# Windowed attention and spectral mixing on one core: the last 64 tokens of v move from GpSimd's queue to SyncE's, as 512-byte rows that four 0/1 products per batch put in place

## The chip, the cores and the metric

The kernel runs on one core of one Trainium2 chip. The metric is the device time of one execution in microseconds, lower is better. Three runs of the kernel before took 447.61, 448.76 and 446.3 us, median 447.61. The profile is of a further execution of 450.29 us.

## What is computed

Attention with 8 heads of 64 over 8 batches of 576 tokens (q, k, v in float32), each token looking at itself and the 127 before it, with a slope per head; its output, 8 x 576 x 512, goes through a Fourier mix with complex weights per mode, and through one dense layer.

```python
B, H, S, D = 8, 8, 576, 64
scores = q @ k.T / sqrt(D) - slope[h] * |i - j|      # where 0 <= i - j < 128, else -1e9
x = softmax(scores) @ v                              # [8, 576, 512], heads side by side
X = rfft(x, axis=1)[:, :64]                          # 64 modes
Y[m] = X[m] @ (w_r[m] + 1j * w_i[m])                 # 512 x 512 per mode, w_r and w_i in float32
u = x + irfft(Y, n=S)
out = u + relu(u @ w_ch)
```

w_r and w_i are 64 x 512 x 512 float32 each, 134 MB together, and are read once.

## The kernel before, in words

**Units and slots.** The attention is done in 32 units: a unit is one batch `b` and one pair of heads `s`. `GROUPS = ((0,), (1, 2, 3))` orders them: first pair 0 for the eight batches (units 0 to 7, group 0), then pairs 1, 2, 3 for batch 0, batch 1 and so on (units 8 to 31, group 1). `_slot(g, n, ...)` (L589) is one step of a software pipeline: scores of unit n, transposes of unit n + 1 on PE (`_tr`, L413) and their evacuation by ACT (`_evac`, L425), casts of q and k of unit n + 2 and of v of unit n + 1 on POOL (`_cast_qk`, L392; `_cast_v`, L401), the spectrum of unit n - 2 (`_spectrum`, L516), the product with v of unit n - 1 (`_av`, L472), and, from unit 8 + 2 on, products with the weights of group 0 (`_pair_of_modes`, L680). The order of the instructions on each engine is the order in which these functions are called; each engine works through its own list in order and waits where a tile is not ready.

**Tokens 512 to 575.** v's first 512 tokens come per unit, in two transfers of 128 KB with 512-byte rows on SP (`_load_v`, L367), and are cast to bf16 (`vb`). The last 64 tokens of all batches are kept in one tile, `vbt` [128, 4 pairs, 8 batches, 72], bf16: partition 64·hh + p holds head hh of the pair and token 512 + p, and a column of ones that gives the sum of the softmax. Before the change they come per pair: `_load_vt` (L378) issues two transfers of 128 KB on GpSimd's queue, in 256-byte rows, and `_cast_vt` (L388) casts 128 x 512 numbers into `vbt`. Pair 0 is loaded after the first cast of q and k and cast before the first transposes; pairs 1 to 3 are loaded in slots 2 to 4 and cast in slots 4 to 6 (L613 to L619). `_av` reads `vbt` in its last two products (L499).

**Loads.** Everything else is issued by SP in one list: q and k of a unit (`_load_unit`, L355, 288 KB each), v of a unit, and weights (`_load_w`, L645). Up to n = 15 this list is written out ahead of everything (L126 to L134): v for units 0 to 4 with their q and k, then v three units behind, and two weight transfers after each unit from 7 on. Later q, k and v are issued from the slots, and weights by `_modes` (L687) as soon as the ring has room. The ring is 12,288 floats per partition, 6 MB: twelve transfers of 512 KB (group 0: 2 modes, 128 rows, w_r or w_i, 64 transfers in all), or four of 1.5 MB (group 1: 384 rows). A transfer needs the room that PE has done with. A transfer also waits until the one eight places ahead of it in SP's list has landed. q and k have 9 buffers each, v 6, vt 2.

**After the attention.** PE goes through the weights of group 1 in order (`_modes`, L704), with the products `u @ w_ch` (`_xw`, L749) and the inverse transform (`_z_early`, L768) between them; `_finish` (L848) puts the results together and writes them out.

**PSUM.** `tqk` of pool `ps1`, two buffers, holds the transposes; `_tr` takes one for q and one for k in each slot:

```python
tp = g.ps1.tile([P, g.R, 64], BF16, tag="tqk", name=f"tqk{w}")
```

**Start.** POOL makes the identity and a few index tiles (`_consts`, L243), DVE makes the distance tile `rel` from them, and ACT the masks (`_mask`, L308), which must be there before the first product with the mask (L464).

Of the kernel before, what the change touches and what calls it, by code (L numbers as in the profile page):

```python
# [9 lines left out]
FP32 = mybir.dt.float32  # L10
BF16 = mybir.dt.bfloat16
# [5 lines left out]
P = 128  # L17
MB = 8
GROUPS = ((0,), (1, 2, 3))
# [4 lines left out]
VB = 6  # L24
# [20 lines left out]
def kernel(  # L45
# [10 lines left out]
    nc = tc.nc  # L56
    B, H, S, D = q.shape
# [4 lines left out]
    g = Ctx()  # L62
# [27 lines left out]
    for b in range(B):  # L90
        t = [(g.x_sb[:, b, st], ((b, st * P), (b, st * P + 64))) for st in range(4)]
        if b % 2:
            t.append((g.x4[:, b // 2], ((b - 1, 4 * P), (b, 4 * P))))
        if b == B - 1:
            t = [t[4], t[1], t[0], t[3], t[2]]
        g.seq += t

    with tc.manual_schedule(engines={ET.SP, ET.PE, ET.Activation, ET.DVE, ET.Pool}):
        with ExitStack() as wctx:
# [5 lines left out]
            with ExitStack() as actx:  # L105
                cp = actx.enter_context(tc.tile_pool(name="const", bufs=1))
                g.Xn[0] = cp.tile([P, 1, 2, B, NM], BF16, name="Xn0")
                g.sel[0] = g.sel[1]
                if JOINT[0] != 2:
                    g.sel[0] = cp.tile([P, JOINT[0], JOINT[0], P], BF16, name="sel0")  # L110
                g.mask = cp.tile([P, NP, 2, 512], BF16)
                g.vbs = [cp.tile([P, 8, 72], BF16, name=f"vb{i}") for i in range(3)]
                g.vbt = cp.tile([P, NP, B, 72], BF16)
                g.qpool = actx.enter_context(tc.tile_pool(name="qk", bufs=QK))
                g.vpool = actx.enter_context(tc.tile_pool(name="v", bufs=VB))
                g.vts = actx.enter_context(tc.tile_pool(name="vts", bufs=2))
                g.work = actx.enter_context(tc.tile_pool(name="work", bufs=2))
                g.ps2 = actx.enter_context(
                    tc.tile_pool(name="ps2", bufs=1, space=bass.MemoryType.PSUM))
                g.ps1 = actx.enter_context(  # L120
                    tc.tile_pool(name="ps1", bufs=2, space=bass.MemoryType.PSUM))
                g.pss = actx.enter_context(
                    tc.tile_pool(name="pss", bufs=1, space=bass.MemoryType.PSUM))

                n0 = g.first[1] + LA
                for n in range(n0):  # L126
                    _load_unit(g, n)
                    if n < VB - 1:
                        _load_v(g, n)
                    elif n >= VB + 2:  # L130
                        _load_v(g, n - 3)
                    if n >= g.first[1] - 1:
                        for _ in range(4 // JOINT[0]):
                            _load_w(g)  # L134
                with tc.tile_pool(name="tmpc", bufs=1, side="right") as tp:
                    _consts(g, tp)
                    _cast_qk(g, 0)
                    for s in GROUPS[0]:
                        _load_vt(g, s)
                    _cast_qk(g, 1)  # L140
                    _cast_v(g, 0)
                    for s in GROUPS[0]:
                        _cast_vt(g, s)
                    _tr(g, 0, 0)
                    _tr(g, 0, 1)
                    _evac(g, 0, 0)
                    _evac(g, 0, 1)
                    first = dict.fromkeys(u[1] for u in units[:2])
                    rest = [s for s in range(NP) if s not in first]
                    for s in first:  # L150
                        _mask(g, tp, s)
                    for n in range(3):
                        _slot(g, n, [], [])
                    for s in rest:
                        _mask(g, tp, s)
                zx = ctx.enter_context(tc.tile_pool(name="zx", bufs=1, side="right"))
                g.ZTa = zx.tile([P, NM // 16, 4, 2, 16, 8], FP32)
                loaded = n0

                work = {n: [] for n in range(N + 2 + TAIL)}  # L160
                for j in range(len(GROUPS) - 1):
                    steps = []
                    for n in range(g.first[j + 1] + 2, g.first[j + 2] + 2):
                        steps += [n] * (SHARE if n < N - LA else SHARE_END)
                    if j + 2 == len(GROUPS):
                        steps += [n for n in range(N + 2, N + 2 + TAIL)] * SHARE_END
                    steps.sort()
                    for m in range(0, NM, JOINT[j]):
                        work[steps[m * len(steps) // NM]].append((j, m))
                for j in set(JOINT):  # L170
                    _sel_rows(g, JOINT.index(j))
                for n in range(3, N + 2 + TAIL):
                    if g.first[1] <= n and loaded < N + 3:
                        if loaded < N:
                            _load_unit(g, loaded)
                        _load_v(g, loaded - 3)
                        loaded += 1
                    w = work[n]
                    h = (len(w) + 1) // 2
                    _slot(g, n, w[:h], w[h:])  # L180
# [62 lines left out]
def _consts(g, tp):  # L243
    nc = g.nc
# [12 lines left out]
    for vb in g.vbs:  # L257
        nc.gpsimd.memset(vb[:, :, g.D : g.D + 1], 1.0)
    nc.gpsimd.memset(g.vbt[:, :, :, g.D : g.D + 1], 1.0)


    pcol = tp.tile([P, 1], FP32)
# [112 lines left out]
            in_=g.v[b, 2 * s + hh, 0:512, :].rearrange("(k p r) d -> p k (r d)", k=2, r=2))  # L375


def _load_vt(g, s):  # L378

    vt = g.vts.tile([P, g.B, g.D], FP32, tag="vt", name=f"vt{s}")  # L380
    for hh in range(2):
        g.nc.gpsimd.dma_start(
            out=vt[64 * hh : 64 * hh + 64],
            in_=g.v[:, 2 * s + hh, 512:576, :].rearrange("b p d -> p b d"))
    g.unit["vt", s] = vt


def _cast_vt(g, s):  # L388
    g.nc.gpsimd.tensor_copy(g.vbt[:, s, :, 0 : g.D], g.unit.pop(("vt", s)))


def _cast_qk(g, n):  # L392
# [196 lines left out]
def _slot(g, n, w0, w1):  # L589


    N = len(g.units)
    if n == g.first[1] + 2:
        _select(g, 0, 0)
    if n < N:
        _score(g, n, 0)
    if n + 1 < N:
        _tr(g, n + 1, 0)
        _evac(g, n + 1, 0)
        _tr(g, n + 1, 1)  # L600
    if n == N + 1:
        _spectrum(g, n - 2)
    for w in w0:
        _pair_of_modes(g, *w)
    if n < N:
        _score(g, n, 1)
    if n + 1 < N:
        _evac(g, n + 1, 1)
    if n + 2 < N:
        _cast_qk(g, n + 2)  # L610
    if n + 1 < N:
        _cast_v(g, n + 1)
    for j, grp in enumerate(GROUPS[1:]):  # L613
        for i, s in enumerate(grp):
            if n == g.first[j + 1] - 4 + i:
                _cast_vt(g, s)
        for i, s in enumerate(grp):
            if n == g.first[j + 1] - 6 + i:
                _load_vt(g, s)  # L619
    if 0 <= n - 2 < N - 1:  # L620
        _spectrum(g, n - 2)
    if 0 <= n - 1 < N:
        _av(g, n - 1)
    if n < N:
        _mask3(g, n)
    for w in w1:
        _pair_of_modes(g, *w)
# [292 lines left out]
```

## Time and profile before

| | |
|---|---|
| median of three runs | 447.61 us (446.3 to 448.76) |
| the profiled execution | 450.29 us |
| its span, first to last instruction of the program | 448.5 us |
| PE / DVE / ACT / POOL busy | 294.1 / 216.1 / 189.6 / 139.1 us |
| moved by DMA | 173.86 MB, 388 GB/s on average |
| of it in POOL's queue (q0, vt) | 1.05 MB |
| granted PE clock, mean | 0.77 |
| vt transfers | 8 of 128 KB, 7.5 us from issue to landing |
| q, k / v transfers | 64 of 288 KB, 6.2 us / 64 of 128 KB, 5.8 us |
| weights | 64 of 1.5 MB (the last one in parts), 13.8 us; 64 of 512 KB, 7.4 to 8.0 us |

How to read it: all times are of one execution and in us from its first instruction. L12 is line 12 of the kernel. The page cuts the span into 40 slices of 11.2 us; a digit is the busy share in tenths. The DMA share is the mean over 16 DMA engines, and can pass 1.0, since the records of packets overlap. "DMA ring<-in_moe_w_r_dram" in a chain is a stretch in which the work waited for that transfer, from its issue to its landing. SPq is SP's list of transfers.

### The profile page before, as it was taken

How to read it: one execution, taken by the hardware profiler on the slowest of the kernel's cores; microseconds unless marked ns; L12 is line 12 of the kernel's file. 1: busy time of each engine (PE TensorE's matmuls, PEld its weight loads, DVE VectorE, ACT ScalarE, POOL GpSimd, SP SyncE). 2: the span in 40 equal slices, each digit the busy share in tenths (PEclk: the TensorE clock that was granted, in tenths of full speed). 3: DMA queues.
4: the chain of work that ended last, by engine and by line, in shares of the span. 5: the costliest groups of instructions: out<-in, count | busy, mean ns of one | idle time of the engine just before them, and what ended most of it. 6: DMA issues, size and time to landing. Idle time of an engine off the chain costs nothing.

```text
span 448.5 us, 12893 instructions
## 1 busy us (share of the span) xinstructions
PE 294.1 (66%) x5506; PEld 204.2 (46%) x5527; DVE 216.1 (48%) x427; ACT 189.6 (42%) x302; POOL 139.1 (31%) x257
## 2 busy tenths in 40 slices
PE   2467989887787885222235664854856748696993
PEld 2455767666666763111123333432433334464661
DVE  8458566566765661010002543453535345462882
ACT  3787656584866741000011331322313233251794
POOL 7699889586876702020000000000000000000700
PEclk9969576686988975555555988589778587899997
DMA  8999999999999999999999999999999999996498
GB/s 249 346 335 327 388 325 353 347 390 379 392 368 375 393 415 429 432 425 426 430 427 433 426 429 429 427 430 426 430 429 430 426 429 430 427 428 282 185 374 288
DMA packets 51562, 173.86 MB, mean 388 GB/s; under 512 B 4912, under 2 KB 21296, under 8 KB 43440
## 3 DMA queue, kind: packets, MB, share of 16 engines
q1 hardware_dynamic: 51120, 171.99, 97.2%
q0 software_dynamic: 384, 1.05, 0.9%
q8 instruction: 43, 0.70, 0.6%
q14 instruction: 15, 0.12, 0.1%
HBM read 163.58 MB, written 9.44 MB: 386 GB/s over the span
## 4 chain that ended last, share of the span: by engine, by line
DMA 50%; PE 26%; ACT 10%; DVE 6%; issue 4%; POOL 2%; ACTq 0%; POOLq 0%
DMA ring<-in_moe_w_r_dram 47%; ACT att L459 6%; PE acc L704 5%; PE sc L447 4%; PE xt L539 4%; PE u L825 3%; PE av L493 3%; DMA ring<-in_moe_w_i_dram 3%; ACT qkT L428 3%; PE tqk L420 2%; PE u L745 2%; POOL qkb L397 1%; PE xw L758 1%; DVE x_sb L507 1%; ACT mask L311 1%
## 5 line engine op out<-in xcount | busy, mean ns | idle before, releaser
L704 PE MATMUL acc<-Xz,ring 128*128 128x32 bf16 x2048 | 70.7, 183 | 100.2 <-DMA ring<-in_moe_w_r_dram 51.0
L704 PEld LDWEIGHTS <-ring 128*128 128x128 bf16 x2048 | 61.3, 101 | 130.1 <-DMA ring<-in_moe_w_r_dram 65.1
L763 ACT CAST hl<-xw 64x512 bf16<-64x512 f32 x72 | 41.7, 579 | 105.6 <-PE xw L758 70.9
L459 ACT ACTIVATE att<-sc 128x1024 bf16<-128x1024 f32 x64 | 65.6, 1025 | 32.8 <-PE sc L447 26.7
L764 DVE TENSOR_TENSOR hl<-xw,hl 64x512 bf16<-64x512 f32 x72 | 49.6, 688 | 58.1 <-ACT hl L763 57.8
L409 POOL CAST vb<-v 64x256 bf16<-64x256 f32 x128 | 64.7, 505 | 20.1 <-PE av L493 13.7
L783 POOL MEMSET ZTa<- 32x512 bf16 x2 | 1.0, 515 | 187.5 <-ACT ZTa L781 187.5
L447 PE MATMUL sc<-qkT,qkT 64*64 64x256 bf16 (+1 forms) x512 | 32.4, 330 | 30.1 <-ACT qkT L428 16.3
L758 PE MATMUL xw<-wch,xT 128*128 128x512 bf16 x138 | 46.3, 467 | 2.7 <-issue 2.2
L428 ACT COPY qkT<-tqk 128x576 bf16<-128x576 bf16 x64 | 40.7, 638 | 0.6 <-PE tqk L420 0.6
L420 PE MATMUL tqk<-ident_b,qkb 64*64 64x64 bf16 x1152 | 31.7, 214 | 7.6 <-POOL qkb L397 6.9
L420 PEld LDWEIGHTS <-qkb 64*64 64x64 bf16 x1152 | 30.8, 130 | 10.2 <-POOL qkb L397 9.2
L464 DVE TENSOR_TENSOR att<-att,mask 128x1024 bf16<-128x1024 bf16 x32 | 26.9, 839 | 14.7 <-ACT att L459 14.5
L585 ACT ACTIVATE Xz<-xz 128x192 bf16<-128x192 f32 (+1 forms) x24 | 7.5, 313 | 59.0 <-DVE Xz L584 57.9
L493 PE MATMUL av<-vb,att 128*128 128x65 bf16 (+1 forms) x512 | 30.8, 215 | 0.6 <-issue 0.2
L584 DVE CAST Xz<-xz 128x384 bf16<-128x384 f32 (+1 forms) x24 | 12.0, 511 | 36.4 <-PE xz L578 35.7
L447 PEld LDWEIGHTS <-qkT 64*64 64x64 bf16 x512 | 13.1, 120 | 35.3 <-ACT qkT L428 18.8
L397 POOL CAST qkb<-k 128x576 bf16<-128x576 f32 x32 | 27.5, 859 | 0.0
L493 PEld LDWEIGHTS <-att 128*128 128x128 bf16 (+1 forms) x512 | 24.4, 111 | 6.5 <-issue 0.6
L397 POOL CAST qkb<-q 128x576 bf16<-128x576 f32 x32 | 24.6, 768 | 6.1 <-PE tqk L420 3.3
L738 DVE COPY xT<-tp 128x512 bf16<-128x512 bf16 x36 | 15.2, 421 | 21.9 <-PE tp L736 21.4
L469 DVE TENSOR_TENSOR att<-att,mask 128x1024 bf16<-128x1024 bf16 x32 | 25.0, 780 | 1.5 <-ACT att L459 1.1
(104 smaller groups left out, 395.2 us busy)
## 6 DMA issues: line engine op xcount, KB each, us to landing
ring<-in_moe_w_r_dram SPq DMA_DIRECT2D x32, 1536.0 KB, 13.8
ring<-in_moe_w_i_dram SPq DMA_DIRECT2D x31, 1536.0 KB, 13.7
ring<-in_moe_w_i_dram SPq DMA_DIRECT2D x33, 512.0 KB, 8.0
ring<-in_moe_w_r_dram SPq DMA_DIRECT2D x32, 512.0 KB, 7.4
q<-in_q_dram SPq DMA_DIRECT2D x32, 288.0 KB, 6.3
k<-in_k_dram SPq DMA_DIRECT2D x32, 288.0 KB, 6.2
v<-in_v_dram SPq DMA_DIRECT2D x64, 128.0 KB, 5.8
out_dram<-o SPq DMA_DIRECT2D x32, 256.0 KB, 3.3
```

Source lines behind the costliest of these rows:

```text
L397: g.nc.gpsimd.tensor_copy(tb, t)
L409: g.nc.gpsimd.tensor_copy(o[64 * r : 64 * r + 64, i], v[64 * i : 64 * i + 64, r])
L420: g.nc.tensor.transpose(tp[hs, r, :], u.b[w][hs, r], g.ident_b[hs, hs], tile_position=(64 * hh, 64 * hh))
L428: g.nc.scalar.copy(dst.rearrange("c (p r) -> c p r", r=g.R), u.tp[w].rearrange("c r p -> c p r"))
L447: nc.tensor.matmul(sc[64 * r : 64 * r + 64, hh, 256 * i : 256 * i + nq], lhsT=kT[hs, c * P + r : c * P + P : 2], rhs=qT[hs, c * P : c * P ...
L459: nc.scalar.activation(a, sc, AF.Exp, scale=1.0 / math.sqrt(g.D))
L464: nc.vector.tensor_tensor(out=a, in0=a, in1=m, op=ALU.mult)
L493: nc.tensor.matmul(av[o, hh, col(t)], lhsT=att[c // 2][:, hh, q0 : q0 + m], rhs=u.vb[:, 2 * c + hh, 0 : D + 1], start=(j == 0), stop=(t < ...
L704: nc.tensor.matmul(acc[:, et, :, m0 - c0 : m0 - c0 + n, :], lhsT=wt[:, a, et * P : (et + 1) * P], rhs=X[:, a, 1 - w : 3 - w, m0 % MB : m0 ...
L758: nc.tensor.matmul(xw, lhsT=xT[:, dt], rhs=g.wch[:, dt], start=(dt == 0 and n in RELU), stop=(dt == 3))
L763: nc.scalar.copy(g.hl[own, n, h], xw[own])
L764: nc.vector.tensor_tensor(out=g.hl[other, n, h], in0=xw[own], in1=g.hl[own, n, h], op=ALU.subtract)
```

## The change

vt comes per batch instead of per pair. `_load_vt(g, b)` issues two transfers of 64 KB on SP, right behind v of the unit with the same number, for b = 0 to 7. Each brings four heads: a row of 512 bytes is two tokens, and lies on partition 4·p + h for tokens 512 + 2p, 512 + 2p + 1 of head h. `_cast_vt(g, b)` casts them to bf16 on POOL (128 x 256 numbers) in slot b, and `_put_vt(g, b)` in slot b + 1 moves them to their places with four products with 0/1 matrices (`selv`, built once by POOL from the identity) into a PSUM tile that takes a `tqk` buffer, from which DVE copies them to `vbt`. `_put_vt` stands ahead of `_spectrum` and `_av` in the slot; `_av` of unit b, in the same slot, is the first to read them. The line numbers of the functions below the change shift by up to 17.

```diff
-                g.vts = actx.enter_context(tc.tile_pool(name="vts", bufs=2))
+                g.vts = actx.enter_context(tc.tile_pool(name="vts", bufs=VB))
+                g.selv = cp.tile([P, 2, 2, P], BF16, name="selv")
...
                     _load_unit(g, n)
-                    if n < VB - 1:
-                        _load_v(g, n)
-                    elif n >= VB + 2:
-                        _load_v(g, n - 3)
+                    for i in [n] * (n < VB - 1) + [n - 3] * (n >= VB + 2):
+                        _load_v(g, i)
+                        if i < B:
+                            _load_vt(g, i)
...
                     _cast_qk(g, 0)
-                    for s in GROUPS[0]:
-                        _load_vt(g, s)
                     _cast_qk(g, 1)
                     _cast_v(g, 0)
-                    for s in GROUPS[0]:
-                        _cast_vt(g, s)
...
+    nc.gpsimd.memset(g.selv, 0.0)
+    src = g.ident_b.rearrange("p (m i h) -> p i h m", i=2, h=2)
+    for r in range(2):
+        for i in range(2):
+            nc.gpsimd.tensor_copy(
+                g.selv[:, i, r].rearrange("p (h m r) -> p r h m", h=2, r=2)[:, r], src[:, i])
...
-def _load_vt(g, s):
-
-    vt = g.vts.tile([P, g.B, g.D], FP32, tag="vt", name=f"vt{s}")
-    for hh in range(2):
-        g.nc.gpsimd.dma_start(
-            out=vt[64 * hh : 64 * hh + 64],
-            in_=g.v[:, 2 * s + hh, 512:576, :].rearrange("b p d -> p b d"))
-    g.unit["vt", s] = vt
-
-
-def _cast_vt(g, s):
-    g.nc.gpsimd.tensor_copy(g.vbt[:, s, :, 0 : g.D], g.unit.pop(("vt", s)))
+def _load_vt(g, b):
+
+    vt = g.vts.tile([P, 2, 2, g.D], FP32, tag="vt", name=f"vt{b}")
+    for i in range(2):
+        g.nc.sync.dma_start(
+            out=vt[:, i].rearrange("p r d -> p (r d)"),
+            in_=g.v[b, 4 * i : 4 * i + 4, 512:576].rearrange("h (p r) d -> p h (r d)", r=2))
+    g.unit["vt", b] = vt
+
+
+def _cast_vt(g, b):
+    t = g.work.tile([P, 2, 2, g.D], BF16, tag="vtb", name="vtb")
+    g.nc.gpsimd.tensor_copy(t, g.unit["vt", b])
+    g.unit["vt", b] = t
+
+
+def _put_vt(g, b):
+
+    t = g.unit.pop(("vt", b))
+    ps = g.ps1.tile([P, 2, 2, g.D], FP32, tag="tqk", name="pvt")
+    for i in range(2):
+        for r in range(2):
+            g.nc.tensor.matmul(
+                ps[:, :, i], lhsT=g.selv[:, i, r], rhs=t[:, :, r], start=(r == 0), stop=(r == 1))
+    g.nc.vector.tensor_copy(
+        g.vbt[:, :, b, 0 : g.D], ps.rearrange("p j i d -> p (j i) d"))
...
-    for j, grp in enumerate(GROUPS[1:]):
-        for i, s in enumerate(grp):
-            if n == g.first[j + 1] - 4 + i:
-                _cast_vt(g, s)
-        for i, s in enumerate(grp):
-            if n == g.first[j + 1] - 6 + i:
-                _load_vt(g, s)
+    if n < g.B:
+        _cast_vt(g, n)
+    if 0 <= n - 1 < g.B:
+        _put_vt(g, n - 1)
```

## The prediction

> **What bounds the kernel now.** I read the page's slices first, then the chain of waits, then the DMA queues, then DMA share and rate in windows of my own.
>
> ```profile
> DMA  8999999999999999999999999999999999996498
> GB/s 249 346 335 327 388 325 353 347 390 379 392 368 375 393 415 429 432 425 426 430 427 433 426 429 429 427 430 426 430 429 430 426 429 430 427 428 282 185 374 288
> ...
> q0 software_dynamic: 384, 1.05, 0.9%
> ...
> DMA 50%; PE 26%; ACT 10%; DVE 6%; issue 4%; POOL 2%; ACTq 0%; POOLq 0%
> ```
>
> The DMA engines are busy in every slice until the last weights land. In the second half they move 425 to 433 GB/s, in the first 325 to 393. So they are never idle, but in the first half they work below their rate. The chain shows the same from 166 us on, where PE waits for weight after weight, up to the last one:
>
> ```profile
> 400.94 0.65 DVE ZTa L780
> 401.60 12.57 DMA ring<-in_moe_w_i_dram
> 414.21 0.28 PE acc L704 x4
> ```
>
> Before 166 us the chain runs over ACT, PE and DVE and shows no transfer, but compute is not what sets the end there. SP issues a transfer when the one eight places earlier has landed: in the trace seven of its transfers are still under way at nearly every issue from 5 to 165 us. The q, k, v and weight stream therefore runs through the attention at the pace of the DMA engines, and the group-1 weights (100.7 MB) follow with no gap. A microsecond of DMA time saved anywhere before 166 us brings every later weight forward by one, as long as the ring has room.
>
> Now the windows (columns after the engines: granted clock, DMA share, GB/s):
>
> ```profile
> 8.00:14.00 6.00, 1.60 (x44) 1.45 (x45) 3.68 (x9) 3.41 (x6) 1.88 (x5) 1.00 1.07 268
> 14.00:28.00 14.00, 7.89 (x209) 6.40 (x209) 7.92 (x19) 12.31 (x20) 12.94 (x22) 0.95 1.05 379
> 28.00:46.00 18.00, 14.55 (x332) 10.96 (x331) 12.42 (x26) 13.40 (x19) 17.05 (x29) 0.78 1.06 315
> 46.00:60.00 14.00, 12.38 (x263) 9.56 (x262) 8.84 (x20) 9.31 (x14) 11.33 (x20) 0.72 1.06 379
> ```
>
> The rate falls to 268 and 315 GB/s in exactly the two stretches in which the vt transfers of POOL's queue are under way (issued 5.6 to 6.4 and 26.3 to 37.7 us, landed 6.7 to 8.1 us later), and is 379 on both sides, at a DMA share just as full.
>
> **The change, part by part.**
>
> *vt leaves POOL's queue.* Beside vt, 8 to 14 us lost (379 - 268) x 6 = 0.67 MB and 28 to 46 us (379 - 315) x 18 = 1.15 MB: 1.82 MB, 4.8 us at 379 GB/s. vt's own 1.05 MB, which count in those rates, are 2.8 us. Together **7.6 us** of DMA time. The floor is the packets alone: 0.9% of the span, 4.0 us. I take 7.6, since the packet records agree: in these windows alone the neighbours' 2304-byte packets (93 ns at the median) stretch.
>
> *vt enters SP's queue:* 16 transfers of 64 KB, 2,048 packets of 512 bytes. The 16,384 such packets of v take 29 ns on average: 2,048 x 29 / 16 engines = **3.7 us**. Lower bound: bytes at 379 GB/s, 2.8 us. Upper: each lands as long after its predecessor as a v transfer of twice the size, 0.36 us, so 5.8 us. I take 3.7, the same packet size.
>
> *SP's issues:* 16 more at 0.48 us apart (q, k, v, v go out at 0.75, 1.20, 1.66, 2.14 us). For units 0 to 4 SP then needs 6 x 0.485 = 2.9 us a unit, and the engines (0.59 + 0.26 + 0.13 MB at 317 to 379 GB/s) 2.6 to 3.1. SP just keeps up: I put 0.4 us on it (0 to 1.5). From unit 5 on the queue is full and issues cost nothing. The q and k behind these issues come later at first: unit 2's q is issued near 6.6 us instead of 4.6. Nobody waits: POOL casts that unit only at 15.2 us now.
>
> *POOL:* gone are eight issues (0.70 each, 5.6 us), four casts (0.64, 2.6) and this wait:
>
> ```profile
> L382 POOL DMA_DIRECT2D vt<-in_v_dram x8: 682/683/830, 5.6 to 37.6; - x8
> L389 POOL CAST vbt<-vt x4: 608/610/747, 14.5 to 46.7; 128x512 bf16<-128x512 f32 x4
> its engine sat idle before it (us, times) until:
>   DMA vt<-in_v_dram: 4.5, 1
> ```
>
> Added: eight casts of 128x256 (between 0.40, a lone vb cast, and 0.64: 4 us), a memset (0.5, by L783) and four copies (0.2 to 0.3, by L336 and L255), partly inside the 1.0 us in which POOL waits for the first q. POOL runs some 4 us earlier, and the 1.9 us that PE waits for its qkb casts between 38.7 and 44.5 us go. What is late next is PE itself.
>
> *PE:* four products of 128x128 by 128 columns in each of slots 1 to 8. The nearest row, four xt products, takes 0.40 us at full and 0.61 at half clock: 0.5 x 8 = 4 us, ahead of `_spectrum` and `_av`. In slots 1, 2 and 6 PE idles 0.3 us before the next scores, which hides about 1 us; with the 1.9 us from POOL, PE ends about 1 us late. The new wait is for vtb: with POOL earlier it is cast a slot ahead; behind it would stand xt, av and the next scores.
>
> *DVE:* eight copies of 128x256 from PSUM (0.41 us, the same shape at L584), 3.3 us, under DVE's 1.1 to 2.8 us waits for av each slot; without that cover, 3.3 us. *Start:* POOL's casts now fall into 10 to 14.5 us, where POOL was idle and DVE finishes `rel` for the first mask (11.97 us). While POOL was casting, L296 took 1.91 us; L294, a shape four times as wide, took 0.28. I allow 0.5 us (0 to 1). PSUM: pvt takes a tqk buffer, but score(n+1, 0) ahead of the next transposes already waits for that buffer's evacuation. The attention thus ends some 1.5 us later (0 to 8, with no cover).
>
> *Does that reach the end?* The first group-1 load is issued at 166.35 us, when PE frees its room, and lands 11.95 us later; its own 1.5 MB take 3.65, so 8.3 us of work stand ahead of it. With the stream 3.5 us earlier, 4.8 are left. The very first q lands 2.96 us after its issue, 2.2 without its own transfer. So room may come about 2.6 us later and no gap opens. 1.5 fits: cost nothing. If the cover goes, each further microsecond is lost.
>
> **Sum:** -7.6 + 3.7 + 0.4 = **-3.5 us**. The profiled execution took 450.29 us (span 448.5 and 1.8 around it), so 446.8 there; the median of the runs is 447.61, so **444.1**. 0.5%, which a measurement of this kernel can tell from no change, is 2.2 us.
>
> **The rivals.**
>
> 1. *Compute eats it.* If PE's, DVE's and POOL's additions do not hide, the attention ends 3.6 to 6 us late, 1 to 3.4 us past the slack, and ring room becomes the limit: about 445.1 to 447.5. For it: PE's clock is at 0.63 to 0.78 from 28 to 90 us, when its added work is dear. Against: the wait rows above. It would show as SP waiting for L704 near 166 us with fewer than four transfers under way. 15%.
>
> 2. *Same engines, same time.* The slow stretches need not come from POOL's queue: 60 to 90 us runs at 340 GB/s with no vt in it. If half the 4.8 us lost by neighbours is small rows as such, and new vt costs 5.8, the sum is -5.2 + 5.8 + 0.4 = +1.0; with 4.5 it is about 0: 447.6. Against: 379 GB/s right before and after, with rows of 512 bytes in it. The Trainium skill, "DMA: Bandwidth & Descriptors", section "Issuing engines are not separate DMA queues", says that transfers started by any engine run on the same 16 DMA engines, so that another issuer only saves issue time; by that alone the time stays. No run here shows it yet, and the dip of the rate speaks for more. 12%.
>
> 3. *Slower: small transfers clog the eight-deep queue.* Each vt takes a place that a q, k or v of 128 to 288 KB had, so less is under way and a straggling DMA engine leaves the others dry. If a vt costs as much as a q (0.73 us between landings), 16 cost 11.7 and the time is 447.6 + 11.7 - 7.6 = 451.7. It turns at 7.6 / 16 = 0.47 us each. For it: 60 to 66 us, with q, k and v alone in the queue, moved only 305 GB/s. Against: v's 0.36 at twice the size. The same page, section "Bandwidth", has 0.95 us for a 64 KB transfer and calls transfers under 64 KB descriptor-dominated; an estimate from that figure is 15.2 us for the 16, some 8 us slower. The trace's landings, 0.36 us apart at 128 KB, disagree as long as they overlap. 13%.
>
> **Numbers.** My forecast has 60%: 444.1, with 441.8 to 445.5 for its own terms (7.6 less 2.8 and a smooth start below; 5.8 at the top leaves -1.4, 446.2, and is least likely). The range reaches over rivals 1 and 2: 441.8 to 448.0; left out are the third and a little below. Faster by over 0.5%: the forecast and a part of rival 1, 0.60. Same: 0.26. Slower: 0.14.
>
> **What would show it.** Right: no software queue in the DMA part; no dip to 268 or 315 GB/s in 8 to 14 and 28 to 46 us; the weights of group 0 issued some 3 us earlier by 60 us; the first 1.5 MB load landing near 174.8 instead of 178.3; the last weight near 410.7 instead of 414.2, with the tail unchanged; `qkb` gone from PE's waits before 45 us. Wrong: rate below 300 GB/s while the 64 KB transfers run (rival 3), a dip that stays (2), or PE rather than DMA on the chain beyond 170 us (1).

## The result, and the profile after

The changed kernel took 451.28 us (median of 21 runs, 448.34 to 455.55), the kernel before 448.15 us (21 runs, 445.75 to 449.81). Two of the 21, over 455 us, count as slow and are left out of the ratio, which compares means: 1.0078, 95% interval 1.0055 to 1.0100, or 3.5 us slower (3.1 by the medians). The forecast was 444.1 with a range of 441.8 to 448.0, so both sign and range were wrong.

The two profiled executions do not show this difference: 450.39 us after, 450.29 before. A second profile of each (e8_after2 and e12_before2 below) has 448.8 and 448.3 us of span. Both profiles of the kernel before are some 2 us above its own median, so the last microseconds of single profiles are not compared here. Positions in the stream of transfers and waits are, and times come from the medians and ratios.

From the page of the changed kernel, the lines that answer to those shown of before:

```profile
DMA  7999999999999999999999999999999999995498
GB/s 236 276 371 333 390 348 341 393 369 390 389 364 398 412 416 430 426 429 426 433 426 430 429 430 426 428 428 431 427 429 431 426 431 426 431 423 237 189 345 312
...
q1 hardware_dynamic: 53424, 173.04, 97.3%
...
DMA 56%; PE 20%; ACT 8%; DVE 5%; SPq 5%; issue 4%; POOL 0%; ACTq 0%; POOLq 0%
```

The software queue is gone, and its 1.05 MB are in q1. From slice 15 on the rates are those of before within a few GB/s, up to the last weights. New is "SPq 5%" in the chain: a twentieth of the span now hangs on SP's own time to issue, which had no share before. The windows (same columns as before: engines, granted clock, DMA share, GB/s):

```profile
8.00:14.00 6.00, 2.53 (x56) 1.75 (x56) 3.31 (x6) 4.68 (x7) 5.66 (x11) 1.00 0.93 272
14.00:28.00 14.00, 9.39 (x222) 7.92 (x223) 8.99 (x21) 12.08 (x19) 13.28 (x25) 1.00 0.94 317
28.00:46.00 18.00, 13.68 (x331) 11.41 (x328) 12.93 (x29) 12.96 (x17) 10.38 (x20) 0.79 0.99 345
46.00:60.00 14.00, 11.06 (x189) 9.12 (x188) 6.83 (x16) 6.86 (x10) 9.43 (x18) 0.50 1.06 386
```

The dip at 28 to 46 us is shallower (345 against 315 GB/s), but a new one has come at 14 to 28 us (317 against 379). Look at the column before the rate: where before had a DMA share of 1.07, 1.05 and 1.06 in the first three windows, there is 0.93, 0.94 and 0.99 now. The slow stretches before were full and slow; these are not full. From 14 to 28 us the share is a tenth lower and the rate a sixth, so the missing share is most of the drop, not all of it. Who holds the engines back, the chain of waits up to 70 us tells:

```profile
by line: DMA q<-in_q_dram 33.6%; SPq L365 10.9%; SPq L385 8.4%; SPq L376 8.0%; DMA v<-in_v_dram 7.3%; ACT att L476 7.2%; issue 3.7%; PE sc L464 3.3%; PE av L510 3.2%; PE xt L556 2.0%; SPq L675 1.7%; POOL qkb L414 1.6%; DVE att L481 1.3%; DV
...
7.35 0.59 SPq L365
7.98 0.43 SPq L365
8.46 0.43 SPq L376
8.93 0.48 SPq L376
9.45 0.55 SPq L385
10.04 0.60 SPq L385
10.69 0.59 SPq L365
...
53.36 0.58 PE pvt L403 x4
```

From 1.7 to 22.7 us the chain is SP issuing transfer after transfer: q, k (L365), v (L376), vt (L385), then the next unit's q 3.34 us after the last one's. A unit's 0.98 MB in 3.34 us are 294 GB/s, an estimate that lies between the 272 and 317 of the first two windows. All of SP's waits from 2 to 28 us are these, 0.8 us (2.0 in the second profile):

```profile
SPq L385 <- DMA q<-in_q_dram: 0.6, 1, 0.6
SPq L385 <- DMA k<-in_k_dram: 0.2, 1, 0.2
```

In the two profiles of before SP waits 7.4 and 7.9 us there, all of it for earlier transfers to land. So in the changed kernel SP is held up by its own issuing, and not by the eight places. The chain goes on over DMA transfers of q, POOL, one transfer of v that lands at 52.9 us, and the products pvt. At the end of the stream the chain hangs on the last weight, as before:

```profile
400.05 12.88 DMA ring<-in_moe_w_i_dram
412.93 0.05 issue
412.98 0.28 PE acc L718 x4
```

A useful place to stand is the ninth weight transfer (of group 0), since by then all vt are loaded in every kernel. It landed at 49.8 and 50.5 us in the two profiles of before, at 51.1 and 51.7 in the two of after. The forecast put it 3.5 us earlier than before; it is 1.2 us later. Where the rest of the loss arises, these four profiles do not show: the 37th weight lands at 137.0 and 135.4 us after, 138.6 and 137.7 before, the last one at 412.9 and 414.6 after, 414.2 and 413.9 before. PE and POOL wait as follows between 11 and 62 us in the changed kernel (us in total, times, longest; two answers):

```profile
PE sc L464 <- ACT att L476: 7.6, 10, 3.1
PE pvt L403 <- POOL vtb L393: 5.3, 3, 1.8
```

```profile
POOL vb L426 <- DMA v<-in_v_dram: 5.2, 3, 2.9
POOL vb L426 <- PE tqk L437: 4.2, 2, 2.5
```

PE waits 5.3 us for the cast vtb (6.3 in the second profile). On POOL that cast stands behind the cast of v, and v of unit 5 lands at 31.8 us and not at 28.7 as before (second profiles: 31.4 and 28.5). Unit 10's first exp comes at 62.5 and 63.0 us, against 58.3 in both profiles of before.

### The profile page after: what moved, and what is told of

It reads as the page before. It is cut to its first block, busy times and chain, and to the rows that moved or that the text cites. A ratio compares the mean times of both kernels' runs of the same rounds, so it can differ in the third digit from the quotient of the medians.

```text
span 448.6 us, 12988 instructions
## 1 busy us (share of the span) xinstructions
PE 298.3 (66%) x5559; PEld 207.5 (46%) x5559; DVE 217.4 (48%) x435; ACT 189.8 (42%) x302; POOL 135.6 (30%) x258
## 4 chain that ended last, share of the span: by engine, by line
DMA 56%; PE 20%; ACT 8%; DVE 5%; SPq 5%; issue 4%; POOL 0%; ACTq 0%; POOLq 0%
DMA ring<-in_moe_w_r_dram 46%; DMA q<-in_q_dram 5%; ACT att L476 5%; PE acc L718 4%; PE sc L464 3%; PE xt L556 3%; DMA ring<-in_moe_w_i_dram 3%; PE u L839 3%; PE av L510 3%; ACT qkT L445 2%; SPq L365 2%; PE u L759 1%; SPq L385 1%; SPq L376 1%; DMA v<-in_v_dram 1%
## 5 line engine op out<-in xcount | busy, mean ns | idle before, releaser
L426 POOL CAST vb<-v 64x256 bf16<-64x256 f32 x128 | 63.0, 492 | 29.9 <-PE av L510 16.2
L772 PE MATMUL xw<-wch,xT 128*128 128x512 bf16 x144 | 47.2, 461 | 0.0
L437 PE MATMUL tqk<-ident_b,qkb 64*64 64x64 bf16 x1152 | 31.4, 216 | 6.3 <-POOL qkb L414 6.2
L481 DVE TENSOR_TENSOR att<-att,mask 128x1024 bf16<-128x1024 bf16 x32 | 27.3, 852 | 14.1 <-ACT att L476 14.0
L414 POOL CAST qkb<-q 128x576 bf16<-128x576 f32 x32 | 25.8, 805 | 5.6 <-PE tqk L437 2.7
L464 PEld LDWEIGHTS <-qkT 64*64 64x64 bf16 x512 | 13.5, 121 | 27.8 <-ACT qkT L445 15.0
L772 PEld LDWEIGHTS <-xT 128*128 128x128 bf16 x144 | 16.6, 116 | 18.2 <-issue 10.2
```

What stands on the lines that cost most here:

```text
L414: g.nc.gpsimd.tensor_copy(tb, t)
L426: g.nc.gpsimd.tensor_copy(o[64 * r : 64 * r + 64, i], v[64 * i : 64 * i + 64, r])
L437: g.nc.tensor.transpose(tp[hs, r, :], u.b[w][hs, r], g.ident_b[hs, hs], tile_position=(64 * hh, 64 * hh))
L464: nc.tensor.matmul(sc[64 * r : 64 * r + 64, hh, 256 * i : 256 * i + nq], lhsT=kT[hs, c * P + r : c * P + P : 2], rhs=qT[hs, c * P : c * P ...
L481: nc.vector.tensor_tensor(out=a, in0=a, in1=m, op=ALU.mult)
L772: nc.tensor.matmul(xw, lhsT=xT[:, dt], rhs=g.wch[:, dt], start=(dt == 0 and n in RELU), stop=(dt == 3))
```

## The experiments

Theory one is about **loads**: SP cannot issue fast enough, and its eight places hold small transfers, so less is under way, v comes late, POOL waits and the new products wait behind POOL. Theory two is about the **products**: casts, products and copies delay the attention by themselves. A third statement is under test as well, that the old dip came from POOL's queue. All times are medians; ratios are of means, against the kernel before run on the same chip (medians 447.6 to 448.2). Runs on different chips are compared by their ratios.

| run | us | ratio, 95% interval |
|---|---|---|
| e1_novt | 443.5 | 0.9906 (0.9876 to 0.9936) |
| e2_noput | 449.1 | 1.0027 (1.0006 to 1.0049) |
| e3_putonly | 448.9 | 1.0033 (1.0011 to 1.0055) |
| e4_sp256 | 448.3 | 1.0009 (0.9986 to 1.0032) |
| e5_spread | 449.7 | 1.0031 (1.0003 to 1.0059) |
| e6_castfirst | 449.9 | 1.0044 (1.0020 to 1.0068) |
| e7_both | 449.3 | 1.0029 (1.0001 to 1.0056) |
| e8_after2 | 450.8 | 1.0073 (1.0041 to 1.0105) |
| e9_earlyv | 449.6 | 1.0036 (1.0008 to 1.0065) |
| e10_all3 | 451.2 | 1.0069 (1.0042 to 1.0095) |
| e11_big | 447.3 | 1.0001 (0.9977 to 1.0025) |
| e12_before2 | 450.1 | a single run |
| e13_two1k | 450.9 | 1.0078 (1.0051 to 1.0104) |
| e14_bignoput | 446.9 | 0.9977 (0.9953 to 1.0000) |
| e15_pool512 | 448.6 | 1.0022 (0.9996 to 1.0047) |
| e16_big16 | 450.3 | 1.0073 (1.0050 to 1.0095) |
| e17_pool_dve | 445.8 | 0.9947 (0.9917 to 0.9978) |
| e18_pool_first | 446.3 | 0.9961 (0.9933 to 0.9988) |

### One part at a time

**e1_novt**: the kernel before with vt neither loaded nor cast (the last 64 tokens of v are left out).

```diff
-    nc.gpsimd.memset(g.vbt[:, :, :, g.D : g.D + 1], 1.0)
+    nc.gpsimd.memset(g.vbt, 1.0)
...
-                    for s in GROUPS[0]:
-                        _load_vt(g, s)
...
-                    for s in GROUPS[0]:
-                        _cast_vt(g, s)
```

> The kernel before with neither the loads nor the casts of vt (the tile is filled with ones, so the last 64 tokens' v is left out). It prices vt in the old form, end to end. If the DMA stream sets the end (theory 'stream'), the 7.6 us that I put on vt's old form all come back: ratio about 0.983 (-7 to -8 us). If attention's compute sets the end as much as the stream does (theory 'compute'), only what POOL's wait and issues cost the slots comes back: -1 to -3 us, ratio 0.993 to 0.998.

The ninth weight lands at 42.0 us, 7.8 and 8.5 us earlier than in the profiles of before. The price of 7.6 us for vt in the stream is right. But the time falls by 4.2 us only, between the two forecasts: the room for the first group-1 weight comes at 164.4 us (166.4 before), and from 166 to 200 us the engines move 400 GB/s where before had 427 (before, then e1_novt):

```profile
166.00:200.00 34.00, 13.38 (x252) 9.06 (x252) 5.27 (x16) 2.49 (x6) 4.73 (x20) 0.50 1.02 427
166.00:200.00 34.00, 12.40 (x256) 8.61 (x255) 4.14 (x13) 1.91 (x5) 4.73 (x20) 0.50 0.99 400
```

A second bound, the end of the attention, lies some 4 us behind the stream. The profile is of the slowest of the eight runs (446.5 us), so its size is rough.

**e2_noput**: the changed kernel without products and copies (vt is loaded and cast, but never put in place).

```diff
-        _put_vt(g, n - 1)
+        g.unit.pop(("vt", n - 1))
```

> The changed kernel with its 16 transfers and its casts, but without the four products and the copy per batch (the values never reach their places). 'Stream' (SP's issues starve the engines at the start): as slow as the changed kernel, +2 to +4 us against before. 'Compute' (the products and copies delay the slots, and weights wait for room): the 3 us go, -2 to 0 us against before.

**e3_putonly**: the kernel before with the four products and the copy added, on zeros and into a spare tile.

```diff
+    if 0 <= n - 1 < g.B:
+        _put_vt(g, n - 1)
```

> The kernel before with vt loaded and cast as it was, plus the four products and the copy per batch on a tile of zeros into a spare tile that nobody reads. 'Stream': no change, within 1 us of before. 'Compute': +2 to +4 us, nearly all of what the change cost.

Each part alone costs something: 0.27% (1.2 us) the loads, 0.33% (1.5 us) the products, together 0.6% of the 0.78%. Both lie between what the two theories asked for. With the loads alone the ninth weight lands at 51.8 us, as late as with everything. So the stream's delay up to there does not come from the products.

**e4_sp256**: the old 256-byte transfers, eight of 128 KB and cast as before, in SP's list (with four vt buffers, not two).

```diff
+                    if n == 0 or 8 <= n < 11:
+                        _load_vt(g, max(0, n - 7))
...
-        g.nc.gpsimd.dma_start(
+        g.nc.sync.dma_start(
```

> The kernel before with its 8 transfers of 128 KB in 256-byte rows put on SP's list (pair 0 behind v of unit 0, pairs 1 to 3 behind v of units 5 to 7), cast as before, no products. 'Stream' with the queue as the cause of the dips: the dips go, half as many issues as the change, -3 to -5 us. 'Stream' with the 256-byte rows as the cause: the dips stay, 0 to -1 us. 'Compute': -2 to -4 us, since POOL is relieved and nothing is added.

The time is that of before, and the dip of the rate in 28 to 46 us is there without any software queue:

```profile
28.00:46.00 18.00, 13.67 (x345) 10.73 (x343) 14.36 (x32) 14.69 (x19) 11.68 (x20) 0.91 1.11 306
```

306 GB/s at a share of 1.11. The dip does not need POOL's queue. That rows of 512 bytes on that queue make none, e15_pool512 shows below.

### Other orders of the same work

**e5_spread**: vt elsewhere in SP's list.

```diff
-                        if i < B:
-                            _load_vt(g, i)
+                    if n in (0, 2, 5, 6, 7, 8, 9, 10):
+                        _load_vt(g, (0, 2, 5, 6, 7, 8, 9, 10).index(n))
```

> The changed kernel with the same sixteen vt transfers elsewhere in SP's list: vt of batches 0 to 7 goes behind unit 0, 2, 5, 6, 7, 8, 9 and 10, so that units 1, 3 and 4 have four issues each as before. Theory one, late loads: in the changed kernel v of units 5 to 7 lands 3.1, 2.2 and 0.8 us later than before, POOL's cast of v waits for it (5.2 us), the cast vtb stands behind that cast, and PE waits 5.3 us for vtb ahead of the products. By it the first weights go out 2 us earlier than in the changed kernel, PE's wait for vtb falls below 2.5 us and the time is about 449 us or less (1.5 to 3 us under the changed kernel). Theory two, the products themselves: 32 products, eight copies and eight casts are paid wherever the transfers stand, and the time is 450.5 us or more. That only SP's issues matter and neither wait does: 450, with PE's wait for vtb as it was.

**e6_castfirst**: vtb cast ahead of v.

```diff
-    if n + 1 < N:
-        _cast_v(g, n + 1)
     if n < g.B:
         _cast_vt(g, n)
+    if n + 1 < N:
+        _cast_v(g, n + 1)
```

> The changed kernel with one pair of lines exchanged: in each slot POOL casts vtb ahead of v, not behind it. The transfers stand where the change put them. Theory one (vtb waits behind a cast that waits for v): PE's 5.3 us of waits for vtb go to under 0.5, unit 10's first exp comes 2 to 4 us earlier than at 62.5 us; but v is as late as before, so the products with v wait in their place and the time falls by 1 to 2 us only, to 449.5 to 450.3. Theory two (the products themselves): the same waits go but the time stays within 0.7 us of the changed kernel's 451.3.

**e7_both**: the two edits together.

> Both edits: the vt transfers spread over units 0 to 10 as in e5_spread, and vtb cast ahead of v. Theory one: no wait for vtb is left, the stream is 2 to 3 us ahead of the kernel before by 135 us, and the time is 446 to 448 us, no slower than the kernel before (448.1). Theory two: the products, casts and copies keep the attention 1.5 us late and the time is 449 to 450, as with the products alone added to the kernel before (448.9).

**e8_after2**: the changed kernel again.

> The changed kernel once more, unchanged: a second profile and more times on the chip of the three above. By theory one PE's waits for vtb come again, 4 to 6 us in slots 5 to 8, and the time is 450 to 452 us. If the waits for vtb are under 2 us here and the time is the same, theory one falls.

The changed kernel's wait for vtb is there again, 6.3 us. e6_castfirst removes it, but a wait for POOL's qkb of 5.1 us takes its place, because POOL still waits 5.9 us for v: 0.9 us gained on e8_after2. Spreading the transfers gained 1.1 us, though the wait for vtb stayed at 5.7 and the first weight was issued at 22.4 us, not earlier than the changed kernel's 21.5: that is the forecast of the third case, in which only SP's issues matter, and a miss of theory one. v of unit 5 lands at 31.9 and 32.3 us in the two spread kernels, no earlier than in the changed kernel. Both edits together gained 1.5 us; 449.3 lies where theory two put it. The intervals of all three overlap with that of e8_after2, so none of these gains is shown.

**e9_earlyv**: v of units 5 to 7 behind their own q and k.

```diff
+                    for i in [n] * (n < VB + 2) + [n - 3] * (n >= VB + 5):
+                        _load_v(g, i)
                     for i in [n] * (n < VB - 1) + [n - 3] * (n >= VB + 2):
-                        _load_v(g, i)
                         if i < B:
                             _load_vt(g, i)
```

> The changed kernel with v of units 5, 6 and 7 put right behind their own q and k in SP's list, not three units later; the vt transfers stay behind units 8, 9 and 10. Nothing is added or taken away. In all four kernels that have vt in SP's queue and the products, POOL waits 3.5 to 10.2 us for v between 11 and 62 us (kernel before: 0.5), and PE's half clock follows its waits. Theory one (late v): POOL's wait for v falls under 2 us, PE's for vtb under 2 us, unit 10's first exp comes by 60 us (changed kernel 62.5 and 63.0), and the time falls by 1 us or more, to 450 or less. Theory two (the products): POOL's wait goes, but PE is as late and the time is above 450.3. Theory three (too few bytes under way at the start): v early only moves the weights back; the first weight lands later than 28.2 us, and the time stays within 0.5 us of the changed kernel.

**e10_all3**: early v, spread vt, vtb first.

> Three edits on the changed kernel: v of units 5 to 7 early, the vt transfers of batches 0 to 7 behind units 0, 2, 4, 6, 8, 9, 9 and 10, and vtb cast ahead of v. If late transfers on POOL's list are the whole loss beyond the products' own price, the time is 446 to 448 us, at or under the kernel before (448.1). If the products with casts and copies are 1.5 us by themselves and the start loses another 1 to 2 us of DMA time to small transfers, it stays at 449 to 450, as the kernel with two of the edits did (449.3).

v of unit 5 lands at 23.3 us in e9_earlyv, but the wait only moves on to unit 8, whose v lands at 49.1: POOL waits 8.2 us for v, PE 4.9 for vtb, and the time falls by 1.2 us, which the intervals do not tell from nothing. The first weight lands at 30.2 us, later than 28.2, as theory three said, though its time, within 0.5 us of the changed kernel, was not met. The sum of three edits is no better than none (451.2, slower than either of its cases said). Moving transfers about in SP's list was not the remedy: in e5, e6, e7, e9 and e10 SP still waits only 1.1 to 1.8 us from 2 to 28 us.

### How many transfers

**e11_big**: one transfer of 128 KB per batch, not two of 64 (1024-byte rows; the placement is left out).

```diff
-    for i in range(2):
-        g.nc.sync.dma_start(
-            out=vt[:, i].rearrange("p r d -> p (r d)"),
-            in_=g.v[b, 4 * i : 4 * i + 4, 512:576].rearrange("h (p r) d -> p h (r d)", r=2))
+    g.nc.sync.dma_start(
+        out=vt.rearrange("p i r d -> p (i r d)"),
+        in_=g.v[b, :, 512:576].rearrange("h (p r) d -> p h (r d)", r=4))
```

> The changed kernel with one transfer of 128 KB per batch, in rows of 1024 bytes (four tokens of one head a partition), in place of two of 64 KB: eight issues fewer. The same products follow on the same shapes, so the tokens land in other places than they belong: the placement is left out. Theory three (SP's issues and its eight places bound the start): in units 0 to 4 SP needs 5 issues or 2.8 us a unit instead of 3.35, the first weight is issued 2 to 3 us earlier than at 21.5 us and lands by 26.5, v of unit 5 lands by 29.5 (changed kernel 31.8 and 31.0), and the time falls by 1 to 1.5 us, to 449.5 to 450. If the bytes and not the number of transfers cost: first weight within 0.7 us of 28.2, time within 0.5 us of the changed kernel.

**e12_before2**: the kernel before, a second profile.

> The kernel before once more, unchanged, for a second profile: its first one took 450.3 us where the median of its times is 448.1. By theory one (late loads and PE's half clock after its waits) the granted clock between 46 and 60 us is above 0.65, as in its first profile (0.72), POOL waits for v under 2 us there, and the last weight lands about 2 us earlier than at 414.2 us. A clock near 0.5 there with a time near 448 would mean that the clock in that window decides nothing.

**e13_two1k**: sixteen transfers of 64 KB with 1024-byte rows, on 64 partitions each (placement left out).

```diff
-            out=vt[:, i].rearrange("p r d -> p (r d)"),
-            in_=g.v[b, 4 * i : 4 * i + 4, 512:576].rearrange("h (p r) d -> p h (r d)", r=2))
+            out=vt[64 * i : 64 * i + 64].rearrange("p i r d -> p (i r d)"),
+            in_=g.v[b, 4 * i : 4 * i + 4, 512:576].rearrange("h (p r) d -> p h (r d)", r=4))
```

> The changed kernel with its sixteen 64 KB transfers kept in number, place and size, but in rows of 1024 bytes on 64 partitions each (the placement is left out, as in e11_big). Both kernels with half as many descriptors per byte; only this one keeps the sixteen issues. Packets: 2,048 of 512 bytes took 27.8 ns each in the changed kernel, 3.6 us over 16 engines; 1,024 of 1024 bytes took 61.1 ns in e11_big, 3.9 us. So rows alone should save nothing. Number of transfers decides: 450 to 451.5 us, four to six transfers under way up to 20 us, group 0's ninth weight transfer landing by 51 to 52 us as in the changed kernel (51.1 and 51.7). Rows or descriptors decide: 447 to 448.5 us and that weight by 49.8 (as in e11_big).

**e14_bignoput**: one transfer per batch, no products (the values are never placed).

> One 128 KB transfer per batch on SP and no products, no copies (the values of vt are never placed: left out). The load part alone, with half the transfers. If number of transfers and products are separate prices, about 1.2 to 1.7 us less than e11_big (447.3): 445.5 to 446.2, which is 2 us or so above the kernel with no vt at all (443.5). If the products cost nothing once the transfers are fewer: 447.

Eight transfers fewer gain 0.72 to 0.77%, or 3.2 to 3.5 us (e11_big against e8_after2 and the changed kernel), more than the 1 to 1.5 expected. The same long rows in sixteen transfers gain nothing (450.9), and their ninth weight lands at 52.6 us. The rows' packets cost the engines no less (1,024 of 61.1 ns against 2,048 of 27.7 ns). Without products, too, eight transfers fewer gain 0.5% (e14_bignoput against e2_noput). In each of these pairs the intervals lie apart. So it is the **number of transfers**. The mean number of SP's transfers under way, from 4 to 8, 8 to 14 and 14 to 28 us, shows the place: 7.6, 8.0, 7.7 before; 6.0, 6.7, 6.7 after; 5.7, 6.7, 7.0 in e13_two1k; 6.9, 7.8, 7.8 in e11_big. And SP, which waits 0.8 us from 2 to 28 us in the changed kernel and 1.1 in e13_two1k, waits 6.8 in e11_big: there it is ahead again, and the eight places are nearly full. e11_big's ninth weight landed at 49.8 us, as expected, though its first weight (27.9) and v of unit 5 (31.8) did not come earlier. Without products it is 446.9: with eight transfers the products cost 0.24%, 1.1 us, which the overlapping intervals do not tell from nothing. In e12_before2 the clock from 46 to 60 us was 0.76, the wait for v 2.0 us; the last weight landed at 413.9, not 2 us earlier.

### Which list

**e15_pool512**: the change's own 64 KB transfers and products, issued by POOL, three batches ahead of their cast.

```diff
-        g.nc.sync.dma_start(
+        g.nc.gpsimd.dma_start(
             out=vt[:, i].rearrange("p r d -> p (r d)"),
...
+    if n + 3 < g.B:
+        _load_vt(g, n + 3)
```

> The change with its own transfers (64 KB, 512-byte rows) and products, but issued on GpSimd's queue as before: batch 0 after the first casts, then three batches ahead of their cast. SP's list is that of the kernel before. If SP's places and issues are what the changed kernel loses: DMA share back at 1.03 or more in 14 to 28 us, ninth weight transfer landing by 47 to 48 us (kernel before 49.8 and 50.5, no vt 42.0), v of unit 5 by 27 us, and a time of 446 to 448.5 us, unless POOL's sixteen issues (0.7 us each, 11 us of POOL in slots 0 to 4) hold its casts up, which shows as PE waiting for qkb or vtb over 5 us. If the software queue itself is what disturbs the neighbours, whatever the row size, the dip of the rate to about 310 to 320 GB/s in 28 to 46 us comes back and the time is 449 or more.

**e16_big16**: the load of e11_big with every token put in its place: sixteen products of 64 columns per batch, vtb first, the 0/1 matrices built after POOL's first casts, and four vt buffers, not six.

```diff
+    tr = t.rearrange("p i r d -> p (i r) d")
+    for s in range(4):
+        for r in range(4):
+            g.nc.tensor.matmul(
+                ps[:, s], lhsT=g.selv[:, s, r], rhs=tr[:, r], start=(r == 0), stop=(r == 3))
```

> A version with right results: one 128 KB transfer per batch in 1024-byte rows on SP, sixteen products of 64 columns per batch that put the tokens in place (twelve more, each with its own weights), vtb cast ahead of v, and the 0/1 matrices built by POOL after its first casts. The load is that of e11_big (447.3 with four products). Each further product is 0.06 to 0.11 us, 0.7 to 1.3 us a slot in slots 1 to 8, 6 to 10 us of PE, of which PE's waits cover some: 448 to 451. At 447.3 or less it would say that PE's time in group 0 is free, and that the products were never a price.

In e15_pool512 the ninth weight lands at 45.5 us: 3.5 us behind the kernel without vt, which is what the 2,048 packets cost, and 5.5 to 6.2 us ahead of the changed kernel with the same transfers. Its windows:

```profile
28.00:46.00 18.00, 13.48 (x285) 11.17 (x275) 11.89 (x25) 11.07 (x15) 17.42 (x30) 0.71 1.05 387
166.00:200.00 34.00, 13.81 (x263) 9.51 (x263) 5.93 (x19) 2.78 (x7) 4.76 (x20) 0.55 0.99 400
```

387 GB/s with 512-byte rows in the software queue, and 393 with no vt at all (e1_novt): no dip, with 0.5 MB of vt landing in this stretch against 0.8 in the kernel before and e4_sp256. With e4_sp256 this puts the dip on the **rows of 256 bytes**, not on the queue that issues them. But POOL is busy 17.42 of 18 us there, PE waits 5.4 us for vtb, the room for the first group-1 weight comes at 167.5 us, and from 166 to 200 us the stream runs at 400 GB/s. A stream 4 to 5 us ahead at the ninth weight was given back at the end of the attention. (This profile is of the slowest of the twelve runs, 451.8 us; the median is 448.6.) e16_big16 adds to PE and moves only 264 GB/s in 14 to 28 us, where SP waits 3.8 us for POOL's vtb to free a vt buffer: 450.3, no gain. So it does not price the added products alone.

**e17_pool_dve**: e15_pool512 with vtb cast by DVE. **e18_pool_first**: e15_pool512 with vtb cast ahead of v, still on POOL.

```diff
-    g.nc.gpsimd.tensor_copy(t, g.unit["vt", b])
+    g.nc.vector.tensor_copy(t, g.unit["vt", b])
```

> The kernel of e15_pool512 (448.6; stream 4.3 us ahead of the kernel before at the ninth weight transfer, but room for the first group-1 weight only at 167.5 us against 166.4) with vtb cast by DVE and not by POOL, eight casts of 0.40 to 0.74 us. In e15_pool512 POOL is 17.4 of 18 us busy between 28 and 46 us and PE waits 5.4 us for vtb. If POOL is what holds the attention up there: PE's waits for vtb under 1.5 us, room at 164 to 166 us, time 446 to 447.6, below the kernel before, with right results. If the price is the products on PE and the copies on DVE: room again at 167 or later and 448.3 or more.

> The kernel of e15_pool512 with vtb cast ahead of v on POOL: the same POOL work in another order. If order is enough: waits for vtb go and the time is 447 to 448. If POOL's amount of work holds the attention up (e17 moves it off POOL, this one does not): PE waits for qkb or av instead and the time stays at 448 to 449.3.

e17_pool_dve has no wait for POOL left on PE in 11 to 62 us, and its group-1 stream has no gap:

```profile
PE sc L465 <- ACT att L477: 11.0, 11, 3.7
PE sc L465 <- ACT qkT L446: 2.0, 2, 1.7
PE av L517 <- DVE vbt L406: 1.3, 2, 0.9
```

```profile
166.00:200.00 34.00, 11.58 (x250) 8.05 (x247) 4.14 (x13) 1.91 (x5) 4.76 (x20) 0.50 1.02 428
```

Room comes at 163.3 us, and the time is 445.8: 0.53% below the kernel before (interval 0.22 to 0.83%), with nothing left out. e18_pool_first is 446.3, not to be told from it, and PE waits for qkb there (2.7 us), but no longer for vtb. So order alone does as much as less work; the other case, that POOL's amount of work holds it up, is not borne out. Both are a little faster than expected, and the intervals of both lie below that of e15_pool512. The products run in both. Beside e1_novt (no vt at all) the whole handling of vt costs 0.41%, 1.8 us, in e17_pool_dve.

## Why the prediction was wrong

The step that failed is the term for **SP's issues**: "SP just keeps up: I put 0.4 us on it (0 to 1.5)". By the ninth weight the same 16 transfers cost 3.5 us of stream on POOL's queue and 9.0 and 9.7 us on SP's, so the term was 5.5 to 6.2 us. Three things were mis-sized in it. A vt issue takes 0.55 to 0.69 us, and the q behind it 0.59, not 0.48, so a unit takes 3.34 us and not 2.9. Six issues a unit then leave fewer than eight transfers under way, some of them small, and a share of 0.93 to 0.99 where 1.05 to 1.07 is full. And "from unit 5 on the queue is full and issues cost nothing" was wrong too: from 28 to 46 us 7.5 transfers are under way, not 7.9, and the share is 0.99 (1.02 in the second profile). Most of the term is there early: the first weight lands at 28.2 and 27.8 us, against 23.8 in e15_pool512. Five units at 3.34 us against 2.6 to 3.1 for the engines give 1.2 to 3.7 us, an estimate; the rest is not broken down.

With that term the sum at the ninth weight is -7.6 + 3.5 + 5.5 to 6.2 = 1.4 to 2.1 us late; 1.2 was measured. This is bookkeeping, not a test, since the term comes from the same landings. The test is e11_big.

A second step failed beside it: the products were put at nothing. At the end of the run the loads alone cost 1.2 us (e2_noput) where the sum said -3.5, and 2.1 to 2.3 us more come with the products and copies (the casts are in both). Of the 3.5 us of lead that were to hide them, 1.6 and 2.2 were there at the 37th weight in the two profiles. That this is why they cost something is argued, not shown: alone in the kernel before they cost 1.5 us as well.

- **vt leaves POOL's queue, -7.6**: the size was right (7.8 and 8.5 by e1_novt). The reason was wrong: rows of 256 bytes, not the software queue (306 GB/s with them on SP, 387 with 512-byte rows on POOL). That the neighbours' packets stretch is true of before (2304-byte packets took 132 and 124 ns on average in the two stretches, 96 to 104 elsewhere) but not needed: in the dip of e4_sp256 they took 96 ns, and its 4,096 packets of 256 bytes, 26.7 ns each, are 6.8 us of the engines by themselves.
- **2,048 packets, 3.7**: right; all 512-byte packets of the changed kernel took 27.7 ns on average, 3.5 us for these, and the stream of e15_pool512 lost 3.5 us to them.
- **The new wait**, "with POOL earlier it is cast a slot ahead": wrong. POOL was not earlier, since v came 3 us later, and PE waited 5.3 and 6.3 us for vtb. The prediction named what is queued behind the products, but not what vtb itself is queued behind on POOL.
- **PE's 4 us and DVE's 3.3**: right as busy time (3.8 and 4.2; 8 x 0.42). As a price they are 0.33% alone in the kernel before, 0.5% on top of the loads, and 0.24%, not clear of noise, in e11_big against e14_bignoput. **Start, +0.5**: nothing; the first exp came at 11.7 us, against 13.05 and 11.8 in the two profiles of before.
- **"So room may come about 2.6 us later and no gap opens"**: comparing first profile with first and second with second, the room came 1.2 us later in one (427 GB/s from 166 to 200 us, no gap) and 2.9 in the other, which then moved 402 GB/s. A gap opened there with only 2.2 us of lead at the 37th weight. In e15_pool512, with 7 to 8 us of lead there, it took nearly all of it.
- **Rival 3** had the direction, the symptom (too little under way) and nearly the time, 451.7, but by luck: its mechanism is not what happened. vt transfers mostly land 0.17 to 0.35 us after their predecessors, far from the 0.47 at which it was to turn, and SP hardly waits for a place (0.8 us). The loss is in what SP has not issued yet. The Trainium skill's 0.95 us for 64 KB ("DMA: Bandwidth & Descriptors", section "Bandwidth") is not what queued transfers showed here.
- **Rival 1** (compute eats it) is true of e1_novt and e15_pool512; here it fits one profile of two. **Rival 2** was right on the cause of the dip: the same 256-byte rows took the same time from SP (448.3) as from POOL. The Trainium skill's section "Issuing engines are not separate DMA queues" ("DMA: Bandwidth & Descriptors"), that another issuer changes only the issue time, agrees with that, and with e15_pool512 too, if one adds that the issue time, which it calls usually small, was the larger part here (5.5 to 6.2 us of stream against 3.5).

What stays open: single profiles scatter by 2 us, and their last weights show no loss, so where the 3.5 us of the ratio end up along the run is not located; that they go with sixteen transfers in SP's list is what the runs show. Nor did I find why the changed kernel regains some 3 us of stream between the ninth and the 37th weight. In both profiles of the changed kernel and those of e5, e6 and e7 the granted clock from 46 to 60 us was 0.50 to 0.61; in the two of before 0.72 and 0.76. Half clock comes after waits of PE there (in the changed kernel PE idles 1.8 us at 39.2, and from 42.0 the clock is 0.5), but e13_two1k had 0.76 and the same time as the changed kernel, so the clock is not shown to be a cause.

## What to carry to other kernels

Before small transfers are added to a list that keeps eight under way, count bytes under way and issues per unit, not only packets: two transfers of 64 KB cost what one of 128 KB did not. Follow a new wait back through the engine that ends it: the producer's queue, and the transfer its neighbour waits for. And when a stream gains, look at once for the second bound; here it lay some 4 us behind, and only with vtb moved off POOL, or ahead of v there, did 1.7 to 2.4 us come through.

## What was not expected of the hardware

An issue of SP took 0.43 to 0.47 us for k and v at the start of the changed kernel, but 0.55 to 0.69 for a vt transfer (128 rows out of four heads), and 0.59 for the q right behind it; why is not shown. GpSimd issued the same transfers in 0.54 to 0.70 us, and they landed 4.7 to 6.0 us after their issue. And 1024-byte packets took 61.1 ns on average (57.6 in e13_two1k) against 27.7 for 512 bytes, so doubling the row saved the engines nothing.
